# Halved first loads and a rewritten order of pieces in an attention and gated-convolution kernel

## The chip, the core and the metric

The kernel runs on one core of a Trainium2 chip. The metric is the device time of one execution in microseconds (us). Five engines work side by side: TensorE (PE in the profile, with its weight loads shown apart as PEld), VectorE (DVE), ScalarE (ACT), GpSimd (POOL) and SyncE (SP), which here does nothing but issue the transfers between main memory and the on-chip memory.

## The reference: what is computed

Four batches of 768 rows; 8 heads of 64. Attention inside a window, with 24 extra columns for block maxima of k and block means of v, feeds a gated convolution layer:

```python
k_sum = k.reshape(B, H, nb, block, D).max(axis=3)
v_sum = v.reshape(B, H, nb, block, D).mean(axis=3)
scores_l = scale * np.matmul(q, k.transpose(0, 1, 3, 2))
mask_l = np.abs(pos[:, None] - pos[None, :]) < window
scores_s = scale * np.einsum('bhsd,bhnd->bhsn', q, k_sum) + np.log(block)
scores_all = np.concatenate([np.where(mask_l, scores_l, -1e9), scores_s], axis=-1)
a = np.exp(scores_all - np.max(scores_all, axis=-1, keepdims=True))
a = a / (np.sum(a, axis=-1, keepdims=True) + 1e-09)
x = np.matmul(a, np.concatenate([v, v_sum], axis=2))      # then (B, S, H * D)
...
for k in range(K):                                        # K = 5
    gate_pre += conv_w[k][None, None, :] * xp[:, k:k + S, :]
gate = 1.0 / (1.0 + np.exp(-gate_pre))
val = x @ w_val
return (gate * val @ w_out).astype(np.float32)
```

## The kernel before

**Units and groups.** The rows are cut into 12 groups of 256 (a group is a batch and a third of its rows). A group has two units, one for each half of the four head pairs (`hp`), so there are 24 units; unit `u` belongs to group `u // 2`. A unit has two head pairs, `r` = 0 and 1.

**The order is written out by hand.** The text `ORDER` names some 1,275 pieces. They are recorded in that order, each engine runs its own pieces in the order in which they stand, and waits for the others by semaphores. A piece is a letter and its unit or group. For a unit: `s` scores (PE, L566, 16 matmul records for each head pair), `n` adds the mask and takes the row maximum (DVE, L581, eight instructions for a unit), `e` exponentials (ACT, L594, eight), `rr` and `rv` row sums and their reciprocals (DVE), `m` multiplies by them (POOL, L608), `t` transposes (PE, L618), `c` copies them out (ACT, or DVE as `cd`), `x` is the product with v (PE, L629 and L647), `Y` and `X` copy x, plain and rounded (ACT; `Yd`, `Xd` on DVE; `Xp` on POOL), `Z` makes the remainder of the rounding (POOL, L669), `I` and `T` are the five taps of the convolution (ACT or DVE `Id`, and DVE L685), `G` the gate (ACT). For a group: `v` is x times w_val (PE, L713), `gf` the gating (DVE), `gh`, `gl` its rounded part and remainder, `o` the product with w_out (PE, L753), `ob` copies it out and `O` stores it.

**What stands at the start.** `W` is a matmul on zeros whose result nobody reads (L335); `wz` clears its operand. `Lk`, `Lq`, `Lv`, `Ln`, `Lwv`, `Lc` load k, q, v, v again turned (vT), the four quarters of w_val and the taps' weights; batch 0 brings the queries of group 0 along with k. `ks` takes the block maxima of k (DVE, L258) and `kc` copies them into the columns that the scores read (POOL, L272). `vp` (DVE, L309) and `vt` (POOL, L318) sum blocks of vT, `vc` copies the sums, `vb` transposes them (PE, L345) and `vbc` puts them into `vblk`, which `x` of group 0 reads beside v. The weights come as 64-bit numbers and are made into 32-bit words: `rb` takes the high half (ACT, L387), `sh` the low bits (DVE, L392), `or` joins them into `wf` (DVE, L400); `wc` and `wl` split `wf` into a rounded part and a remainder. The scores of all units share one pair of PSUM banks, so `s` of a unit waits until all eight `n` of the unit before have read it. Group 0 multiplies by `wf` itself, in eight pieces of four matmul records; later groups use the two parts. `F` copies block means into a group's v by four small transfers (L369), and waits on SP until that v has landed.

Of the kernel before, what the change touches and what calls it, by code (L numbers as in the profile page):

```python
# [10 lines left out]
F32 = mybir.dt.float32  # L11
# [47 lines left out]
vp1.1 n1.1.1 e1.1.1 n1.0.0 n1.0.1 e1.0.1 t0.1 W33 c0.1 e1.0.0 orwv0 vp0.1 vp1.0 vp0.0 rr1 m0.0
t0.0 vt2.0 vc0.1 vc1.0 vt2.1 s2.1 s2.0 vc0.0 vc1.1 orc rv1 vb0 m1.0 n2.0.0 n2.1.1 n2.0.1 n2.1.0  # L60
c0.0 e2.0.0 e2.0.1 rbwv1 t1.0 e2.1.1 e2.1.0 c1.0 shwv1 vbcd0 orwv1 s3.0 s3.1 rbwv2 Lk1.0 x0.1
x0.0 Y0 m1.1 vt2.2 wcpwv0 wlwv0 t1.1 v0.1.0.0 n3.0.0 n3.1.1 n3.1.0 rr2 shwv2 n3.0.1 orwv2 I0.1
T0.1.0 rv2 T0.1.1 ks1.0 e3.0.0 e3.1.0 I0.0 e3.1.1 e3.0.1 c1.1 vt3.0 vt3.1 vt3.2 vt3.3 vt3.4
vc3.0 vt2.3 vt2.4 vc2.1 m2.1 vc3.1 vc2.0 m2.0 kc1.0 Lq2 s4.1 s4.0 Lwv3 Lv1 Lk1.2 Lk1.1 T0.1.2
n4.0.0 n4.1.0 n4.0.1 T0.0.0 n4.1.1 T0.0.1 shwv3 rr3 v0.0.1.0 v0.1.1.0 vb1 t2.1 e4.1.0 vbc1 s5.1
s5.0 T0.1.3 rv3 n5.1.0 T0.0.2 n5.0.0 T0.0.3 e4.0.0 e4.1.1 c2.1 rbwv3 x1.0 x1.1 Lk1.3 G0 Y1
# [60 lines left out]
v9.0.1 v9.0.0 T19.0.3 n23.0.1 T19.1.0 n23.1.1 e23.1.1 Xd21 rr22 T19.1.1 T19.1.2 T19.1.3 e23.0.1
# [14 lines left out]
def tile_attention_then_gated_conv(  # L142
# [746 lines left out]
```

## Time and profile before

| what | value |
|---|---|
| median of 3 runs | 234.44 us (234.27 to 234.57) |
| the profiled execution: its time, and its span | 233.49 us, 231.7 us |
| busy: PE, PEld, DVE, ACT, POOL | 97%, 83%, 86%, 71%, 73% of the span |
| moved by DMA | 46.20 MB |
| TensorE clock granted, mean | 0.998 of full |

The span is the stretch from the first to the last instruction in the trace; the 1.8 us between it and the execution's own time lie around it. Busy shares are means over the whole span, and a matmul's record is longer than its share of a run of matmuls, because they overlap; how fast PE goes is read from the distance between starts, or from the length of a run divided by its count.

### The profile page before, as it was taken

The numbers are of one execution on the slowest core, as the hardware profiler recorded it, in microseconds if no ns is written. First come the engines' busy times: TensorE is split into PE (matmuls) and PEld (weight loads), VectorE is DVE, ScalarE is ACT, GpSimd is POOL, SyncE is SP. The second block draws the span as 40 slices with busy tenths as digits, with TensorE's granted clock in tenths as the row PEclk, the third lists the DMA queues.
The fourth block names the chain that finished last, engine by engine and source line by source line (L and its number), as shares of the span: only waits on it lengthen the run. The fifth ranks groups of instructions, "written<-read, shape, count | busy, mean of one in ns | idle before, by whom it ended". The sixth has DMA issues, their size and how long they took to land.

```text
span 231.7 us, 8482 instructions
## 1 busy us (share of the span) xinstructions
PE 224.4 (97%) x3210; PEld 191.9 (83%) x3210; DVE 199.7 (86%) x743; ACT 165.4 (71%) x564; POOL 169.0 (73%) x257
## 2 busy tenths in 40 slices
PE   7988999999999999999999999999999999999994
PEld 2457798985798889998898898889998899879884
DVE  3699999999999999999999999978999987887610
ACT  2499999999999998689895575964856792543211
POOL 3289998888898989999989895884572945547220
PEclk9999999999999999999999999999999999999999
DMA  6999899999693983996834356102747230001052
GB/s 246 380 419 413 319 335 327 367 305 361 246 315 76 340 271 100 355 312 184 253 94 171 133 171 187 42 11 74 239 143 233 48 141 0 3 0 48 0 226 91
DMA packets 16167, 46.20 MB, mean 199 GB/s; under 512 B 2272, under 2 KB 2528, under 8 KB 16128
## 3 DMA queue, kind: packets, MB, share of 16 engines
q1 hardware_dynamic: 16128, 45.67, 57.0%
q8 instruction: 25, 0.41, 0.8%
q14 instruction: 14, 0.11, 0.2%
HBM read 37.21 MB, written 6.29 MB: 188 GB/s over the span
## 4 chain that ended last, share of the span: by engine, by line
PE 83%; DVE 11%; ACT 3%; issue 1%; POOL 0%; ACTq 0%; DVEq 0%; POOLq 0%
PE out L753 28%; PE val L713 25%; PE s L566 8%; PE pt L618 8%; PE x L629 7%; DVE g L685 4%; PE warm_out L335 3%; DVE sn L581 2%; PE x L647 2%; DVE wf L400 1%; DVE vpad L309 1%; ACT gt L692 1%; DVE ks L258 1%; PE vsp L355 1%; DVE gf L721 1%
## 5 line engine op out<-in xcount | busy, mean ns | idle before, releaser
L685 DVE SCALAR_TENSOR_TENSOR g<-xf,cwt,g 128x256 f32<-128x256 f32 x192 | 93.3, 486 | 7.3 <-ACT g L219 3.0
L594 ACT ACTIVATE p<-sn,nm 128x120 f32<-128x120 f32 x192 | 73.5, 388 | 8.9 <-DVE nm L581 7.6
L608 POOL TENSOR_TENSOR p<-p,ri 128x480 f32<-128x480 f32 x48 | 46.7, 987 | 14.6 <-DVE ri L604 11.6
L713 PE MATMUL val<-xh,wv 128*128 128x256 f32 x352 | 49.6, 284 | 0.0
L581 DVE CUSTOM_DVE_ANT_0 sn<-s,mask 128x120 f32<-128x120 f32 x192 | 43.7, 276 | 3.4 <-PE s L566 3.4
L753 PE MATMUL out<-wo,gh 128*128 128x512 f32 (+1 forms) x184 | 45.8, 390 | 0.3 <-ACT gh L726 0.3
L713 PEld LDWEIGHTS val<-xh,wv 128*128 128x128 f32 x352 | 44.3, 189 | 0.9 <-issue 0.2
L753 PEld LDWEIGHTS out<-wo,gh 128*128 128x128 f32 x184 | 32.4, 188 | 7.3 <-ACT gh L726 0.7
L669 POOL TENSOR_TENSOR xl<-xf,xh 128x512 fp32r<-128x512 f32 x22 | 28.2, 1287 | 12.6 <-ACT xh L656 6.9
L594 ACT ACTIVATION_READ_ACCUMULATOR p<-sn,nm 128x1 f32 x192 | 36.8, 192 | 0.0
L729 POOL TENSOR_TENSOR gl<-gf,gh 128x512 fp32r<-128x512 f32 x22 | 28.2, 1289 | 7.6 <-ACT gh L726 7.3
L621 ACT COPY pts<-pt 120x512 f32<-120x512 f32 x42 | 23.6, 578 | 10.1 <-PE pt L618 10.1
L692 ACT ACTIVATE gt<-g 128x512 f32<-128x512 f32 x24 | 14.3, 597 | 19.7 <-DVE g L685 19.7
L618 PE MATMUL pt<-ident,p 128*120 128x128 f32 x192 | 26.7, 274 | 1.3 <-POOL p L608 1.3
L713 PE MATMUL val<-xl,wv 128*128 128x256 f32 x176 | 27.6, 279 | 0.0
L286 POOL TENSOR_TENSOR vT<-vT 128x384 f32<-128x384 f32 (+3 forms) x44 | 25.0, 569 | 2.9 <-DMA vT<-in_vT_dram 0.3
L618 PEld LDWEIGHTS pt<-ident,p 128*120 128x120 f32 x192 | 21.7, 137 | 5.1 <-POOL p L608 2.2
L753 PE MATMUL out<-wo,gl 128*128 128x512 f32 (+1 forms) x92 | 23.8, 381 | 0.0
L566 PE MATMUL s<-k,q 64*64 64x120 f32 x704 | 23.3, 267 | 0.3 <-DVE g L685 0.3
L713 PEld LDWEIGHTS val<-xl,wv 128*128 128x128 f32 x176 | 23.6, 188 | 0.0
L566 PEld LDWEIGHTS s<-k,q 64*64 64x64 f32 x704 | 18.2, 133 | 3.0 <-issue 2.2
L219 ACT ACTIVATE ob<-out 128x512 f32<-128x512 f32 (+1 forms) x21 | 11.9, 574 | 11.2 <-PE out L753 7.2
(83 smaller groups left out, 327.5 us busy)
## 6 DMA issues: line engine op xcount, KB each, us to landing
v<-in_vw_dram SPq DMA_DIRECT2D x24, 512.0 KB
vT<-in_vT_dram SPq DMA_DIRECT2D x16, 384.0 KB
out_dram<-ob SPq DMA_DIRECT2D x23, 256.0 KB
k<-in_kT_dram SPq DMA_DIRECT2D x12, 478.0 KB
q<-in_qT_dram SPq DMA_DIRECT2D x11, 512.0 KB
k<-in_kq_dram SPq DMA_DIRECT2D x4, 606.0 KB
raw_wv<-in_wv_dram SPq DMA_DIRECT2D x4, 512.0 KB
raw_wo<-in_wo_dram SPq DMA_DIRECT2D x4, 512.0 KB
```

Source lines behind the costliest of these rows:

```text
L286: nc.gpsimd.tensor_tensor(dst, src[:, :, :n], src[:, :, n : 2 * n], ALU.add)
L566: nc.tensor.matmul(sp(u)[64 * e : 64 * e + 64, h, c * KW : c * KW + KW], qs[64 * h : 64 * h + 64, i * QT : i * QT + QT], ktile[b, pr][64 * ...
L581: nc.vector.tensor_tensor_reduce(sn(u)[:, n, :], sp(u)[:, h, c * KW : c * KW + KW], mask[:, mv, :], -1.0 / math.sqrt(D), 3.0e38, ALU.add, ...
L594: nc.scalar.activation(pr_(u)[:, n, :], sn(u)[:, n, :], AF.Exp, bias=nm(u)[:, n : n + 1], scale=-1.0, accum_out=rs(u)[:, n, 0:1],)
L608: nc.gpsimd.tensor_tensor(pr_(u)[:, w], pr_(u)[:, w], st["ri", u][:, w].unsqueeze(2).broadcast_to([P, TPU, KW]), ALU.mult,)
L618: nc.tensor.transpose(pt[:KW, i, :], pr_(u)[:, TPU * r + i, :], ident)
L621: (eng or nc.scalar.copy)(pts(u)[:, TPU * r : TPU * r + TPU], st.pop(("pt", u, r))[:KW])
L669: nc.gpsimd.tensor_tensor(xl(g)[:, two(hp), :], xf(g)[:, two(hp), HALO:], xh(g)[:, two(hp), :].bitcast(F32), ALU.subtract,)
L685: nc.vector.scalar_tensor_tensor(gp(u)[:, r], xf(g)[:, pr, o : o + SG], cwt[:, pr, o : o + 1], gp(u)[:, r], ALU.mult, ALU.add,)
L713: nc.tensor.matmul(pp[:, r], w, x, start=first and n == 0, stop=last and n == len(terms) - 1)
L729: nc.gpsimd.tensor_tensor(gl(g)[:, two(cp), :], grp["gf", g, cp], gh(g)[:, two(cp), :].bitcast(F32), ALU.subtract)
L753: nc.tensor.matmul(pp, x, w, start=start and n == 0, stop=stop and n == len(terms) - 1)
```

## The change

The loads of v of group 0 and of q of group 1 are each split by `hp`, so that unit 0 and unit 2 need only a first half. The low bits of one quarter of w_val are taken on POOL (`shpwv1`), by a multiplication and a minimum in place of a shift. `v0_sum` gets a parameter that no piece sets. All pieces stand in another order; there is one `W` less, and some copies and first taps change their engine. The matmuls that give results are the same.

```diff
 ORDER = """
-ez wz W0 W1 W2 W3 W4 W5 Mu Lk0.0 Lk0.1 Mm ks0.0 ks0.1 kc0.0 W6 W7 W8 W9 W10 W11 W12 W13 W14 W15
...
+ez hal0 Mu wz W0 W1 W2 W3 W4 W5 W6 W7 W8 W9 W10 W11 W12 Mm Lk0.1 ks0.1 Lk0.0 ks0.0 Mi kc0.1
...
-    def load_q(g):
+    def load_q(g, hp=None):
         b, th = divmod(g, NTH)
+        if hp is not None:
+            nc.sync.dma_start(qt(g)[:, two(hp)], qT[b, th][:, two(hp)])
+            return
         nc.sync.dma_start(qt(g), qT[b, th])
...
-    def load_v(g):
+    def load_v(g, hp=None):
         b, th = divmod(g, NTH)
-        t = ld.tile([VROWS, TPU, DM], F32, tag="v", name=f"v_{g}")
+        if g not in vtile:
+            vtile[g] = ld.tile([VROWS, TPU, DM], F32, tag="v", name=f"v_{g}")
+        t = vtile[g]
+        if hp is not None:
+            for e in range(VP):
+                nc.sync.dma_start(t[:, 2 * e : 2 * e + 2, half(hp)], vw[b, th, e][:, :, half(hp)])
+            return
...
     def low_bits(eng, dst, raw):
         low = raw.rearrange("p (n two) -> p two n", two=2)[:, 0]
+        if eng is nc.gpsimd:
+            eng.tensor_scalar(dst.bitcast(U32), low, 2.0**-29, 7.0, ALU.mult, ALU.min)
+            return
         eng.tensor_scalar(dst.bitcast(U32), low, 29, None, ALU.logical_shift_right)
```

**The loads.** SyncE's rows after the four loads of k (which stand first in both kernels), before the change; `wv0` to `wv3` are the quarters of w_val, `vT_0_2` is vT of batch 0 and head pair 2, `v_0` and `q_1` belong to groups 0 and 1:

```order
L451 DMA cwraw_177<-in_cw_dram 128x40
L415 DMA raw_wv0_179<-in_wv_dram 128x1024
L292 DMA vT_0_1_181<-in_vT_dram 128x768
L292 DMA vT_0_0_183<-in_vT_dram 128x768
L292 DMA vT_0_2_185<-in_vT_dram 128x768
L230 DMA q_1_187<-in_qT_dram 128x1024
L415 DMA raw_wv1_189<-in_wv_dram 128x1024
L249 DMA v_0_191<-in_vw_dram 128x1024 x2
L415 DMA raw_wv2_194<-in_wv_dram 128x1024
L292 DMA vT_0_3_196<-in_vT_dram 128x768
```

And of the change, in the same place:

```order
L300 DMA vT_0_1_177<-in_vT_dram 128x768
L300 DMA vT_0_0_179<-in_vT_dram 128x768
L300 DMA vT_0_3_181<-in_vT_dram 128x768
L462 DMA cwraw_183<-in_cw_dram 128x40
L231 DMA q_1_185<-in_qT_dram 128x512
L426 DMA raw_wv1_187<-in_wv_dram 128x1024
L426 DMA raw_wv0_189<-in_wv_dram 128x1024
L255 DMA v_0_191<-in_vw_dram 128x2x256 x2
L231 DMA q_1_185<-in_qT_dram 128x512
L426 DMA raw_wv2_320<-in_wv_dram 128x1024
L300 DMA vT_0_2_322<-in_vT_dram 128x768
L233 DMA q_2_324<-in_qT_dram 128x1024
```

The vT loads and half of q move up, v of group 0 comes with half its bytes; its other half follows behind `wv3`.

**PE behind x of unit 0.** PE's rows from that place on, before; `pt_1_1` is the transpose of unit 1 and head pair 1, `val_0_1` a piece of group 0's product with w_val, `s_4` the scores of unit 4:

```order
L618 MATMUL pt_1_1_438<-ident_100,p_1_278 120x128 x4
L713 MATMUL val_0_1_443<-xf_0_263,wf_108 128x256 x2
L566 MATMUL s_4_497<-k_0_1_130,q_2_495 64x120 x8
L566 MATMUL s_4_497<-k_0_0_128,q_2_495 64x120 x8
L713 MATMUL val_0_0_539<-xf_0_263,wf_108 128x256 x2
L713 MATMUL val_0_1_443<-xf_0_263,wf_108 128x256 x2
L345 MATMUL vb_1_544<-ident_100,vpad_103 128x128 x4
```

And of the change, behind x of unit 0:

```order
L577 MATMUL s_3_425<-k_0_3_175,q_1_185 64x120 x8
L577 MATMUL s_3_425<-k_0_2_173,q_1_185 64x120 x8
L629 MATMUL pt_1_0_451<-ident_100,p_1_275 120x128 x4
L724 MATMUL val_0_1_466<-xf_0_117,wf_108 128x256 x4
L724 MATMUL val_0_0_471<-xf_0_117,wf_108 128x256 x2
L629 MATMUL pt_1_1_474<-ident_100,p_1_275 120x128 x4
L577 MATMUL s_4_492<-k_0_1_144,q_2_324 64x120 x8
L577 MATMUL s_4_492<-k_0_0_148,q_2_324 64x120 x8
```

Three pieces of the product stand ahead of the scores of unit 4, where one stood (two rows are one piece); the scores of unit 3 stand behind x of unit 0 and stood ahead of it.

**DVE between the scores of units 2 and 3.** DVE's rows before; `sn_2` and `nm_2` are the masked scores and the maximum of unit 2:

```order
L581 ISA sn_2_347,nm_2_348<-s_2_320,mask_99 128x120
L581 ISA nm_2_348 128x1
L392 TENSOR_SCALAR wf_108<-raw_wv1_189 128x512
L222 TENSOR_SCALAR vb_105<-vb_0_341 120x2x256
L400 SCALAR_TENSOR_TENSOR wf_108<-sc_wv1_363,wf_108 128x512
L581 ISA sn_3_446,nm_3_447<-s_3_379,mask_99 128x120
```

And of the change:

```order
L592 ISA sn_2_348,nm_2_349<-s_2_302,mask_99 128x120
L592 ISA nm_2_349 128x1
L403 TENSOR_SCALAR wf_108<-raw_wv0_189 128x512
L615 RECIPROCAL ri_1_399<-ri_1_399 128x8
L411 SCALAR_TENSOR_TENSOR wf_108<-sc_wv0_374,wf_108 128x512
L411 SCALAR_TENSOR_TENSOR wf_108<-sc_wv1_376,wf_108 128x512
L671 COPY xf_0_117<-x_0_0_356 128x2x256
L403 TENSOR_SCALAR wf_108<-raw_wv2_320 128x512
L592 ISA sn_3_460,nm_3_461<-s_3_425,mask_99 128x120
```

Both quarters that the first pieces need are joined here, one of their low bits comes from POOL, the put into `vblk` has gone to ACT, and the copy of x has come from ACT.

## Rows read from the trace of the kernel before

**Rows 1.** The page: busy time by engine, and the costliest group (busy us, mean ns).

```profile
PE 224.4 (97%) x3210; PEld 191.9 (83%) x3210; DVE 199.7 (86%) x743; ACT 165.4 (71%) x564; POOL 169.0 (73%) x257
...
L685 DVE SCALAR_TENSOR_TENSOR g<-xf,cwt,g 128x256 f32<-128x256 f32 x192 | 93.3, 486 | 7.3 <-ACT g L219 3.0
```

**Rows 2.** The chain in order of time: start us, us, what.

```profile
17.68 0.20 DVE sn L581
...
24.80 1.05 PE s L566 x32
...
216.04 1.42 PE val L713 x12
217.46 11.05 PE out L753 x60
228.58 0.38 ACT ob L219
```

**Rows 3.** PE's timeline: start us, us; in brackets idle before it.

```profile
1.53 6.77 PE L335 MATMUL warm_out<-warm 128*128 128x512 bf16 x22 [1.53 <-POOL warm L330]
8.23 0.64 PE L566 MATMUL s<-k 64*64 64x120 f32 x16
...
20.30 0.33 PE L647 MATMUL x<-pts,v 120*64 120x64 f32 x2
...
22.58 0.65 PE L618 MATMUL pt<-ident,p 128*120 128x128 f32 x4
23.32 1.13 PE L713 MATMUL val<-xf,wf 128*128 128x256 f32 x4
...
33.08 2.76 PE L713 MATMUL val<-xf,wf 128*128 128x256 f32 x12
...
36.64 1.05 PE L566 MATMUL s<-k,q 64*64 64x120 f32 x32
```

**Rows 4.** The timeline of PE's weight loads: the last slow one, then the quick ones.

```profile
4.91 0.15 PEld L335 LDWEIGHTS <-warm 128*128 128x128 bf16 x1 [0.28 <-issue]
5.33 2.47 PEld L335 LDWEIGHTS <-warm 128*128 128x128 bf16 x12 [0.27 <-issue]
```

**Rows 5.** DVE's timeline.

```profile
5.76 0.95 DVE L258 TENSOR_REDUCE ks<-k 128x24 f32<-128x768 f32 x1 [0.53 <-DMA k<-in_kq_dram]
8.94 0.28 DVE L581 CUSTOM_DVE_ANT_0 sn<-s,mask 128x120 f32<-128x120 f32 x1 [2.23 <-PE s L566]
...
19.02 0.89 DVE L392 TENSOR_SCALAR wf<-raw_wv 128x512 uint32<-128x512 uint32 x1
19.83 0.68 DVE L222 TENSOR_SCALAR vb<-vb 120x512 f32<-120x512 f32 x1
20.43 0.68 DVE L400 SCALAR_TENSOR_TENSOR wf<-sc_wv,wf 128x512 uint32<-128x512 uint32 x1
```

**Rows 6.** ACT's timeline.

```profile
21.84 0.65 ACT L387 ACTIVATE sc_wv<-raw_wv 128x512 f32<-128x512 f32 x1
```

**Rows 7.** POOL's timeline.

```profile
1.51 0.53 POOL L195 IOTA lag<- 128x120 f32 x3
...
13.67 1.93 POOL L608 TENSOR_TENSOR p<-p,ri 128x480 f32<-128x480 f32 x2 [0.68 <-DVE ri L604]
...
40.91 2.53 POOL L669 TENSOR_TENSOR xl<-xf,xh 128x512 fp32r<-128x512 f32 x2 [0.70 <-ACT xh L656]
```

**Rows 8.** POOL's groups by line: busy us, mean ns of one, idle before.

```profile
L440 POOL TENSOR_TENSOR wv<-wf,wv 128x512 fp32r<-128x512 f32 x4 | 5.1, 1274 | 0.2
...
L437 POOL CAST wv<-wf 128x512 fp32r<-128x512 f32 x4 | 2.4, 610 | 0.0
```

**Rows 9.** Windows: us, busy PE, PEld, DVE, ACT, POOL, PEclk, DMA share, GB/s.

```profile
20.00:25.00 5.00, 4.56 (x96) 3.60 (x92) 5.00 (x25) 4.81 (x20) 4.41 (x7) 1.00 1.04 421
...
25.00:45.00 20.00, 20.00 (x333) 17.66 (x327) 19.77 (x91) 19.20 (x71) 18.67 (x35) 1.00 0.93 336
...
165.00:185.00 20.00, 20.00 (x294) 18.10 (x294) 19.07 (x63) 13.35 (x49) 12.03 (x15) 1.00 0.56 171
```

**Rows 10.** SyncE's timeline: time to issue.

```profile
28.93 3.46 SPq L369 DMA_DIRECT2D v<-vb  x4
```

More of the change, by code (lines that the diff above doesn't have):

```diff
@@ new lines @@
+s12.1 T6.0.1 rr10 rv10 T6.0.2 T6.0.3 Y8 ob2.1 Ya8 n12.0.1 tv2.3 Z6 m9.1 o2.0 Z7 Lu2.1 Lk3.3
+Lk2.2 ks2.2 ks2.3 kc2.3 kc2.2 O1.1 Lu2.2 Lv5 F5 t9.1 t9.0 v3.0.1 v3.1.0 G6 e11.1.0 X8 I7.0 c9.1
+e11.0.0 e12.0.1 c9.0 e11.0.1 x9.1 Id7.1 T7.0.0 n12.1.1 T7.0.1 n12.1.0 T7.1.0 n12.0.0 T7.0.2
+T7.1.1 T7.0.3 T7.1.2 T7.1.3 e11.1.1 e12.0.0 tv2.2 hal4 s13.0 x9.0 Y9 m10.1 Z8 Ya9 m10.0 G7 Lk3.0
+Lk3.1 O1.0 s13.1 n13.0.0 n13.1.0 v3.0.0 I8.0 gf3.0 Id8.1 v3.1.1 t10.0 t10.1 X9 Z9 n13.0.1 T8.0.0
+rr11 e12.1.0 e12.1.1 rr12 T8.0.1 T8.0.2 n13.1.1 gf3.1 T8.1.0 T8.1.1 T8.1.2 rv11 c10.0 c10.1
@@ new lines @@
+c12.1 Xp11 tv3.3 Z11 Z10 gl4.0 s16.0 s16.1 x12.1 x12.0 e14.0.1 e14.1.0 e14.0.0 ob3.0 T10.0.3
+rr14 m13.1 n16.1.1 n16.1.0 n16.0.1 G10 e15.1.1 I11.0 Y12 e15.0.1 m13.0 ks3.2 rv14 Ya12 n16.0.0
+Xd12 m14.1 v5.1.0 v5.0.1 t13.1 t13.0 v5.0.0 ob3.1 e15.1.0 I11.1 c13.0 cd13.1 x13.1 x13.0 Y13
+T11.1.0 T11.0.0 T11.0.1 T11.1.1 T11.1.2 kc3.0 gl4.1 m14.0 hal6 Z12 s17.0 s17.1 e15.0.0 e16.0.0
+gf5.0 T11.1.3 Ya13 T11.0.2 T11.0.3 n17.0.1 ks3.3 rr15 X13 G11 v5.1.1 o4.1 I12.1 I12.0 n17.1.1
+T12.0.0 T12.1.0 T12.1.1 T12.0.1 T12.0.2 rv15 T12.0.3 n17.1.0 gf5.1 Z13 tv3.2 ob4.1 t14.0 t14.1
@@ new lines @@
+o4.0 m15.0 v6.0.1 v6.1.1 v6.0.0 m15.1 kc3.3 n17.0.0 T12.1.2 cd14.1 T12.1.3 gh5.0 e16.1.0 e16.1.1
+e17.0.1 e17.1.1 gh5.1 e16.0.1 gl5.0 gl5.1 kc3.2 e17.1.0 G12 cd14.0 I13.0 I13.1 ks3.1 kc3.1
+T13.0.0 T13.0.1 T13.1.0 gf6.0 t15.1 c15.1 Lv8 F8 O3.1 O3.0 Lq10 Lu3.1 Lq9 Lv7 F7 Lu3.0 O0.0
+tv3.1 t15.0 c15.0 s18.0 s18.1 x14.0 x14.1 Y14 n18.1.1 n18.0.0 e17.0.0 ob4.0 e18.1.1 n18.0.1
+e18.0.1 e18.0.0 Ya14 T13.1.1 T13.0.2 rr16 rv16 n18.1.0 T13.1.2 o5.1 x15.0 x15.1 s19.1 s19.0
+v6.1.0 ob5.1 T13.0.3 Yd15 rr17 Ya15 T13.1.3 G13 e18.1.0 tv3.0 hal7 ghp6.0 m16.1 m16.0 I14.0
@@ new lines @@
+t16.1 t16.0 c16.1 I14.1 n19.1.0 n19.0.1 n19.1.1 gf6.1 rr18 T14.1.0 T14.1.1 rv17 T14.1.2 n19.0.0
+T14.1.3 T14.0.0 c16.0 X14 o5.0 x16.1 x16.0 s20.0 s20.1 e19.1.0 e19.0.1 Y16 e19.0.0 hal8 Xd15
+gl6.0 m17.1 ghp6.1 Z14 gl6.1 Ya16 n20.0.1 m17.0 T14.0.1 n20.1.1 n20.1.0 rv18 T14.0.2 T14.0.3 G14
+o6.0 t17.1 t17.0 vsp3 c17.0 n20.0.0 cd17.1 Z15 Xp16 s21.0 s21.1 x17.1 x17.0 e20.0.1 ob5.0
+e20.0.0 vscd3 e19.1.1 Id15.0 Id15.1 T15.1.0 T15.1.1 T15.1.2 m18.0 T15.0.0 Y17 Ya17 T15.1.3
+T15.0.1 T15.0.2 T15.0.3 rr19 G15 v7.0.0 v7.1.0 v7.1.1 v7.0.1 m18.1 t18.1 t18.0 O4.0 Lv9 O4.1 F9
@@ new lines @@
+rv19 n21.0.1 n21.1.1 gf7.1 ob6.0 Lv10 O5.1 Lq11 F10 O6.0 e20.1.0 I16.0 e20.1.1 Id16.1 T16.0.0
+rr20 T16.0.1 T16.1.0 rv20 T16.1.1 T16.1.2 c18.0 c18.1 Xp17 hal9 Z17 Z16 v8.0.0 v8.1.1 x18.0
+x18.1 e21.1.1 Y18 T16.1.3 T16.0.2 m19.1 m19.0 T16.0.3 m20.1 n21.1.0 G16 Ya18 I17.1 v8.1.0 v8.0.1
+t19.0 t19.1 I17.0 n21.0.0 T17.0.0 gf8.0 e21.0.1 c19.0 c19.1 s22.1 s22.0 x19.0 x19.1 e21.1.0
+e21.0.0 T17.1.0 gf7.0 ghp7.0 T17.1.1 T17.1.2 T17.0.1 T17.0.2 n22.1.1 T17.0.3 Xp18 m20.0 gh7.1
+gl7.1 gl7.0 n22.1.0 T17.1.3 Y19 Ya19 rr21 G17 gf8.1 n22.0.1 I18.0 o6.1 o7.0 t20.1 t20.0 o7.1
@@ new lines @@
+I18.1 e22.1.1 c20.0 e22.0.1 c20.1 T18.0.0 T18.0.1 rv21 T18.1.0 m21.1 obd7.0 n22.0.0 T18.0.2
+T18.1.1 Xd19 hal10 ghp8.0 m21.0 gl8.0 Z18 Z19 T18.1.2 t21.0 t21.1 c21.0 c21.1 gh8.1 gl8.1 s23.1
+s23.0 T18.1.3 T18.0.3 G18 I19.0 obd7.1 I19.1 x21.1 x21.0 Y21 n23.0.0 T19.0.0 T19.0.1 n23.0.1
+T19.1.0 x20.1 x20.0 Y20 T19.1.1 T19.1.2 T19.1.3 T19.0.2 T19.0.3 v9.1.0 o8.1 v9.1.1 X20 e23.0.1
+e22.0.0 obd8.1 e22.1.0 n23.1.0 rr22 rv22 O5.0 ob6.1 O6.1 O7.0 O7.1 Lv11 F11 X21 G19 Id20.1
+n23.1.1 e23.1.1 T20.1.0 v9.0.0 v9.0.1 T20.1.1 e23.1.0 I20.0 T20.0.0 e23.0.0 T20.0.1 rr23 T20.0.2
@@ L138 @@
+gf11.0 T23.1.3 v11.1.1 v11.1.0 ghp11.0 G23 gl11.0 o10.0 O9.0 ob10.0 O8.0 O8.1 gf11.1 ob10.1
+ghp11.1 gl11.1 o11.0.1 obd11.0.1 O11.0.1 O10.1 O9.1 O10.0 o11.1 ob11.1 O11.1 o11.0.0 ob11.0.0
+O11.0.0
 """
```

136 lines of the change are left out of this document (48 added, 88 removed).

## The prediction

> **What bounds the kernel now.** I read the busy shares first: PE has work in 97% of the span, DVE in 86% [rows 1]. A mean over stages with different limits says little, so the windows came next: from 25 us on PE is busy in all of the stretches shown, 20.00 of 20.00 us [rows 9]. Then the chain: it enters PE for good at 24.80 with the scores of unit 4, and its last stretch on PE is 11.05 us of the output product from 217.46 on; after that only a copy at 228.58 and a store are left [rows 2]. So the end is the moment from which PE is never short of work, plus the PE work still to do, plus some 3 us of copy and store. No result-giving matmul is added or removed, so the question is how much of that work PE has done when it stops starving.
>
> What starves it before 24.80? PE's timeline begins with 22 matmuls on zeros, 1.53 to 8.23, and only then come the first scores [rows 3]. DVE, idle for 2.23 us, begins masking them at 8.94 [rows 5] and from there has no gap: five of five us in the window 20 to 25 [rows 9]. PE waits for its results: x of unit 0 from 20.30, the first piece of group 0's product at 23.32, the scores of unit 4 at 24.80 [rows 2, 3].
>
> **Part 1: the first scores.** In the order of the change 13 of the matmuls on zeros, not 22, stand ahead of them, and the operand is cleared behind POOL's iota (0.53 us [rows 7]), so they start some 0.55 later, at 2.08. The weight loads show two paces: at 4.91 and 5.33 the starts are 0.42 apart, from 5.33 on 12 take 2.47, 0.21 each [rows 4]: 512 columns at 1.2 and at 2.4 GHz. Nine were slow (1.53 to 5.33, 3.8 us). With nine slow and four quick ones: 2.08 + 3.8 + 4 x 0.21 = 6.7, with a first weight load 6.8, against 8.23. The first of the two k blocks has been reduced by 5.2 (the reduction of the second waits for its load until 5.76 [rows 5]) and put in place by POOL at 5.7, so it isn't late. DVE can mask from about 7.45 (scores 0.57, a semaphore 0.1), **1.5 us earlier**.
>
> **Part 2: DVE up to the scores of unit 4.** These wait for all eight maskings of unit 3. Before, DVE took 24.80 - 8.94 = 15.86 us. In that run the change takes out the low bits of one quarter (0.81 from start to start, 19.02 to 19.83), the put into `vblk` (0.60, 19.83 to 20.43) [rows 5] and one join (0.60, it stands later now), and puts in the copy of x (taken as 0.60, like the put of the same 512 columns). Maskings at 0.20 [rows 2], reductions, block sums and two taps are the same. 15.86 - 0.81 - 0.60 - 0.60 + 0.60 = 14.45. Walked piece by piece, DVE also waits about 1.0: 0.3 around the first maskings, 0.4 for x of unit 0, 0.3 for the scores of unit 3. 7.45 + 14.45 + 1.0 = 22.9.
>
> **Part 3: PE up to there.** x of unit 0 needs four things. Its transposes: POOL's multiplication starts 12.1 (13.67 before [rows 7], less the 1.5). The block sums: DVE has them at 14.85, POOL's copies at 15.75, the transposes on PE at 16.25, ACT's put at 16.9. The half of v: 5.52 MB stand up to it in the queue, 6.30 before; the second k block (1.24 MB) had landed by 5.76 [rows 5] and the rate is 421 GB/s [rows 9], so it lands near 5.76 + 4.28 / 0.421 = 15.9 instead of 17.8. The put is the last, so x runs from 16.95, not 20.30, for 2.1 (20.30 to about 22.4 [rows 3]). Then scores of unit 3 (0.98), a transpose (0.45), three pieces of the product, of which 12 records take 2.59 (33.08 to the next group [rows 3]; 0.86 a piece), another transpose (0.5): 19.05 + 0.98 + 0.45 + 2.6 + 0.5 = 23.6. DVE is ready at 22.9, so unit 4's scores start at **23.6**, with three pieces done where one was: 24.80 - 23.6 + 2 x 0.86 = **2.9 us ahead**. The same walk to the scores of unit 6 (36.64 before [rows 3]) has DVE ready at 33.55 and PE there at 33.7 with the same seven pieces done: 2.9 again.
>
> **Prices that no row shows.** The low bits on POOL: a cast of 512 columns takes 0.61, a two-operand operation 1.27 [rows 8]; the bounds are nothing (if hidden) and twice the dearer, 2.5. I take 1.0, as it has one operand but two operations. It starts near 16.3; its join on DVE also waits for two conversions on ACT (0.57 each, from one of 0.65 with overlap [rows 6]) which end at 18.5, so up to 2.2 it costs nothing, and beyond that it delays the first pieces one for one: 0 to 0.3. The half loads: pieces of 1 KB in place of 4 KB a partition. From below nothing; from above the poorer 336 GB/s at a share of 0.93 in 25 to 45 [rows 9], 361 at full share, makes 1.05 MB cost 2.9 instead of 2.5. I take 0.2 for the first half; the load has 1.0 to spare against the put, so nothing. By the Trainium skill ("DMA: Bandwidth & Descriptors", section Bandwidth) halving is a loss: a transfer of 1 MB reaches 341 GB/s and one of 64 KB 138, so batch to 1 MB or more; an estimate at the smaller figure would make the 0.52 MB land 2.5 us later and x of unit 0 start near 18.5. The rows disagree: 384 to 512 KB transfers queued one behind the other run at 421 GB/s here [rows 9]. Block means for group 1 (`F`): v of group 1 stands at 9.8 MB, landing near 26.1, then 3.46 to issue [rows 10], landed by 31; x of unit 2 comes at 34.7. Hidden, with 3.7 to spare.
>
> **Part 4: from there to the end.** POOL must give remainders of x in time for group 1's product. Before, the two ended at 40.91 + 2.53 = 43.4 [rows 7], and the product, begun 42.5, needs the second about 0.95 later: just in time. In the change POOL starts 1.57 earlier, sheds two casts (1.2 [rows 8]) and two copies of k maxima (0.8), had idle time of 1.2, and gains the low bits (1.0): 3.8 earlier, about 39.6 to 40.2, where PE begins at 38.7 and needs it at 39.65. I take **0.4 lost** (0 to 0.6). Later DVE has 0.93 idle in 165 to 185 and 0.23 in 25 to 45 [rows 9], and a dozen first taps go from it to ACT: it can follow. For small waits in the new order 0.1. The end, copy and store, is as long as before.
>
> Sum: 2.9 - 0.4 - 0.1 = 2.4. Against its own execution 233.49 - 2.4 = 231.1. That stands 0.95 under the median of the runs, so I forecast **232.0** for the median. A difference of 0.2% (0.47 us) is about what can be told from none.
>
> **The rivals.**
> - *The lead can't be kept* (0.14). DVE and POOL are 99% and 93% busy in 25 to 45 [rows 9], and they start only 1.5 earlier. If PE must fall back to them, the gain is 1.5 less the 0.4 and 0.1: 1.0, 233.4. Against it: the walk has DVE ready before PE at units 4 and 6, because pieces left it.
> - *POOL is as late as it was* (0.08). If the low bits and what was moved about it leave the remainders at 43.4, the product of group 1 starts no earlier and nothing is gained: 234.4, no change. It needs POOL to lose 3.8 us, against a dearest price of 2.5.
> - *The clock* (0.05). PEclk reads 1.00 in the rows, but the pace doubled only at 5.33 [rows 4]. If it doesn't double in the first 10 us now, the 13 take 5.5, scores take 0.8 and the eight before unit 1's scores are slow too: these come at 12.6 instead of 10.0, and 0.2 of the gain is left, 234.2. Against: PE is busy from 2.08 to 9.7 almost without a gap.
> - *Slower: the taps at the end* (0.11). Behind x of unit 23 PE has four whole output products (2.76 each: 11.05 is worth four) and four pieces at 1.42 [rows 2] before the last gated part is read, and 0.95 more before its remainder is: 17.6 us. In that time DVE has 18 taps at 0.49 [rows 1], four first taps (0.5), four gatings and a copy (0.6), then come a gate (0.6), a cast (0.61) and a remainder (1.27 [rows 8]), with 0.6 for semaphores: 16.8. A backlog B at that point costs B - 0.8, and from B = 3.7 the kernel is slower than before; with 4.3 it takes 235.5. For it: 0.93 idle in 20 us is little [rows 9]; against: taps have gone to ACT, busy 13.35 of 20.
> - Otherwise as forecast (0.62): 230.9 to 233.0. The lower end is the full 3.35 by which x of unit 0 moves, with 0.2 on top.
>
> **How the numbers follow.** Faster: the forecast, and the first rival, 0.62 + 0.14 = 0.76. Same: POOL and the clock, 0.13. Slower: 0.11. The range runs from 230.9 up to 234.4, which takes in all but the slower case and a bit below.
>
> **What would show it.** Part 1: the first scores near 6.8, DVE's first masking near 7.45. Part 2: POOL's operation on the low bits under 2.2 and no wait of the join. Part 3: x of unit 0 from 16.95 without a wait for v, the scores of unit 4 near 23.6 with three pieces ahead. Part 4: PE's wait in group 1's product under 0.6, and the last output matmul 2.4 earlier than before. I am wrong if PE's waits behind 25 us come to more than 1 us, on POOL's remainders, on the scores held by DVE, or on the last gating; or if the first scores come after 7.6.

## The result: slower by 1.0 to 1.7%, where a gain of 1% was forecast

The change takes 236.90 us (median of 4 runs, 236.37 to 238.13), and the kernel before, run between them on the same chip, 234.50 us (median of 4, 234.27 to 238.76). The ratio is 1.0136, 95% interval [1.0101, 1.0170]: 2.4 to 4.0 us slower; the two medians lie 2.4 apart. The prediction was 232.0 us, with 0.76 on faster. The profiled execution took 236.37 us, its span is 234.3. Ratios, this one and those below, are against runs of the kernel before on the same chip, and leave out an execution that took over 1.5% longer than the fastest of its kernel, as the 238.76 here.

**Busy time and PE's waits.** The page of the change (busy time), which answers to [rows 1], then its waits of PE (us in total, times, longest):

```profile
PE 224.9 (96%) x3209; PEld 192.1 (82%) x3209; DVE 199.4 (85%) x738; ACT 167.5 (71%) x568; POOL 171.1 (73%) x258
```

```profile
PE s L577 <- DVE nm L592: 1.0, 2, 0.6
PE val L724 <- DVE xf L671: 0.8, 1, 0.8
PE val L724 <- POOL xl L680: 0.4, 1, 0.4
PE x L658 <- DMA v<-in_vw_dram: 0.4, 1, 0.4
PE pt L629 <- ACT pts L632: 0.4, 1, 0.4
```

PE and DVE do as much as before; ACT and POOL do 2.1 us more each, of 234. What is longer is the time in which PE has nothing to do (9.4 us of its span, 7.3 before); behind its start, 3.4 of that are waits of 0.2 to 0.8 (2.2 before).

**The chain in order of time**, for [rows 2]:

```profile
2.89 7.19 DMA vT<-in_vT_dram
10.09 8.41 DMA v<-in_vw_dram
...
21.85 0.69 DVE xf L671
...
149.98 1.50 DVE xh L667
...
213.39 1.27 POOL xl L680
```

Before, it was on PE from 24.80 until the taps near the end. Now it starts with two loads, and leaves PE again at 20.2 and near 142. The load of v that ends at 18.50 is the half that unit 0 waits for. The end is alike in both: the prediction has the chain before enter PE "for good" at 24.80, but between the rows of [rows 2] it left it once more, for taps and gatings from 187.91 on, and came back at 207.07:

```profile
187.91 0.60 ACT ob L219
...
206.40 0.63 ACT gh L726
```

In the change it is off PE near the end from 207.53 to 214.70.

**PE's timeline**, for [rows 3]:

```profile
2.14 5.25 PE L343 MATMUL warm_out<-warm 128*128 128x512 bf16 x13 [2.14 <-POOL warm L338]
7.32 0.64 PE L577 MATMUL s<-k 64*64 64x120 f32 x16
...
17.29 0.33 PE L658 MATMUL x<-pts,v 120*64 120x64 f32 x2
...
18.55 0.34 PE L658 MATMUL x<-pts,v 120*64 120x64 f32 x4 [0.39 <-DMA v<-in_vw_dram]
...
20.15 1.05 PE L577 MATMUL s<-k,q 64*64 64x120 f32 x32
...
22.59 2.86 PE L724 MATMUL val<-xf,wf 128*128 128x256 f32 x12 [0.81 <-DVE xf L671]
...
25.82 1.05 PE L577 MATMUL s<-k,q 64*64 64x120 f32 x32
...
31.41 1.05 PE L577 MATMUL s<-k,q 64*64 64x120 f32 x32 [0.59 <-DVE nm L592]
...
37.06 1.05 PE L577 MATMUL s<-k,q 64*64 64x120 f32 x32
```

The scores of unit 4 start at 25.82 (24.80 before [rows 2]), with three pieces of the product done where one was: 2 x 0.86 - 1.02 = 0.7 us ahead, not 2.9. At the scores of unit 6 (37.06 against 36.64 [rows 3], seven pieces done in both) PE is 0.4 behind.

**The pace**, for [rows 4]: the last slow weight load on zeros, and the first scores after it.

```profile
6.38 0.15 PEld L343 LDWEIGHTS <-warm 128*128 128x128 bf16 x1 [0.28 <-issue]
6.79 0.10 PEld L343 LDWEIGHTS <-warm 128*128 128x128 bf16 x1 [0.26 <-issue]
7.32 0.41 PEld L577 LDWEIGHTS s<-k 64*64 64x64 f32 x16 [0.42 <-issue]
```

Here eleven starts lie 0.43 apart (512 columns at 1.2 GHz), where before nine did, so the first scores came 0.5 later than forecast.

**DVE, ACT and POOL about x of unit 0**, for [rows 5], [rows 6] and [rows 7]; three timelines:

```profile
8.03 0.28 DVE L592 CUSTOM_DVE_ANT_0 sn<-s,mask 128x120 f32<-128x120 f32 x1 [0.91 <-PE s L577]
...
17.52 0.42 DVE L403 TENSOR_SCALAR wf<-raw_wv 128x512 uint32<-128x512 uint32 x1
...
18.45 1.33 DVE L411 SCALAR_TENSOR_TENSOR wf<-sc_wv,wf 128x512 uint32<-128x512 uint32 x2 [0.40 <-ACT sc_wv L395]
21.85 0.69 DVE L671 COPY xf<-x 128x512 f32<-128x512 f32 x1 [2.06 <-ACT g L219]
```

```profile
20.26 0.45 ACT L219 ACTIVATE g<-x,cwt 128x256 f32<-128x256 f32 x1 [0.47 <-PE x L660]
20.63 0.38 ACT L605 ACTIVATE p<-sn,nm 128x120 f32<-128x120 f32 x1
...
21.39 0.43 ACT L219 ACTIVATE g<-x,cwt 128x256 f32<-128x256 f32 x1
```

```profile
12.89 1.93 POOL L619 TENSOR_TENSOR p<-p,ri 128x480 f32<-128x480 f32 x2 [0.90 <-DVE ri L615]
...
16.96 1.97 POOL L401 TENSOR_SCALAR wf<-raw_wv 128x512 uint32<-128x512 uint32 x1
```

x of unit 0 is done by 20.2, and DVE is free at 19.8; yet it copies x only at 21.85, behind the *second* of ACT's two taps on the same x (21.39 + 0.43). Between the two taps ACT does two exponentials. All three instructions only read x, but they read one PSUM tile from two engines, and the copy stands behind the taps in the order: it carries a wait for ACT. Before, ACT made the copy itself, first. The low bits on POOL took 1.97, twice the 1.0 taken.

**The windows**, for [rows 9], in the stretch with the least room, and SyncE's row that answers to [rows 10]:

```profile
25.00:45.00 20.00, 18.81 (x302) 16.09 (x301) 20.00 (x80) 18.69 (x67) 16.78 (x26) 1.00 0.85 306
```

```profile
28.78 3.96 SPq L377 DMA_DIRECT2D v<-vb  x4
```

DVE is busy in all of the 20 us, and PE, which was busy in 20.00, is now so in 18.81. Issuing the block means took 0.5 longer, and no wait of PE follows from it.

### The profile page after: what moved, and what is told of

It reads as the page before. It is cut to its first block, busy times and chain, and to the rows that moved or that the text cites. A ratio compares the mean times of both kernels' runs of the same rounds, so it can differ in the third digit from the quotient of the medians.

```text
span 234.3 us, 8466 instructions
## 1 busy us (share of the span) xinstructions
PE 224.9 (96%) x3209; PEld 192.1 (82%) x3209; DVE 199.4 (85%) x738; ACT 167.5 (71%) x568; POOL 171.1 (73%) x258
## 4 chain that ended last, share of the span: by engine, by line
PE 73%; DVE 10%; DMA 7%; ACT 6%; POOL 1%; issue 1%; SPq 1%; DVEq 0%; ACTq 0%
PE val L724 26%; PE out L764 25%; PE pt L629 7%; PE x L640 6%; PE s L577 6%; DMA v<-in_vw_dram 4%; DVE g L696 3%; DMA vT<-in_vT_dram 3%; ACT p L605 2%; PE x L658 2%; DVE sn L592 2%; SPq L238 1%; ACT g L219 1%; ACT pts L632 1%; ACT xf L671 1%
## 5 line engine op out<-in xcount | busy, mean ns | idle before, releaser
L740 POOL TENSOR_TENSOR gl<-gf,gh 128x512 fp32r<-128x512 f32 x22 | 28.7, 1307 | 5.5 <-ACT gh L737 5.0
L764 PEld LDWEIGHTS out<-wo,gl 128*128 128x128 f32 x92 | 16.9, 188 | 3.4
```

The source lines that it names most:

```text
L740: nc.gpsimd.tensor_tensor(gl(g)[:, two(cp), :], grp["gf", g, cp], gh(g)[:, two(cp), :].bitcast(F32), ALU.subtract)
L764: nc.tensor.matmul(pp, x, w, start=start and n == 0, stop=stop and n == len(terms) - 1)
```

## The experiments

To compare kernels whose orders differ, PE's result-giving matmuls were added up in each trace, each with the mean distance between starts of its kind. The table gives by how many us a kernel reaches the same sum later than the kernel before (- is earlier), at the moments named above. Where kinds of matmul stand in another sequence it swings by some tenths. Its early columns also hold something that is not the order's: the moment at which PE's pace doubles differs from one execution to the next, from 4.5 to 8.1 us in the fourteen traces, and with it the first scores, which came at 6.43 to 7.80 with the start of the change and at 7.84 to 9.10 with that of before. e4, at 7.79, is one of the late ones.

```
                                 25     30     36     45     60    110    140    170    225 us
change                         -0.6   -0.7   +0.5   +0.8   +0.8   +0.8   +1.4   +2.0   +2.1
e1 copy first                  -2.1   -1.7   -1.0   -0.8   +0.3   +0.4   +1.2   +1.8   +1.9
e2 v first                     -0.2   -0.3   +1.2   +1.6   +1.6   +1.6   +2.1   +2.7   +2.8
e3 bits on DVE                 -0.7   -0.8   +0.4   +0.9   +0.9   +0.9   +1.7   +2.5   +2.7
e4 all three                   -1.2   -1.2   +0.4   +0.7   +0.7   +0.7   +1.6   +2.3   +2.5
x1 start of change             -0.7   -0.7   +0.8   +2.0   +1.8   +1.6   +1.6   +1.8   +1.8
x2 rest of change              -0.3   -0.4   -0.4   +1.0   +1.5   +0.8   +1.5   +2.2   +2.3
x3 best start, then before     -2.4   -2.0   -0.1   +0.8   +0.5   +0.3   +0.3   +0.5   +0.5
b1 halves alone                +0.5   +0.9   +0.9   +0.8   +0.5   +0.5   +0.5   +0.5   +0.6
x4 change up to 113            -1.0   -1.1   +0.1   +0.5   +0.5   +0.5   +4.2   +4.4   +4.4
x5 change from 110             -0.1   +0.2   +0.2   +0.2   +0.9   +0.9  +11.9  +12.6  +12.7
x7 rounding on ACT             -0.4   -0.4   +1.1   +1.4   +1.4   +1.4   +2.0   +2.0   +2.2
```

**The copy ahead of the taps.** One piece of the change is moved:

```diff
-s3.1 s3.0 e2.1.1 I0.1 e2.0.0 I0.0 e2.1.0 t1.0 rbwv2 Yd0 shwv2
+s3.1 s3.0 e2.1.1 Yd0 I0.1 e2.0.0 I0.0 e2.1.0 t1.0 rbwv2 shwv2
```

> One piece of the changed kernel moves: DVE's copy of x of unit 0 stands ahead of ACT's first taps, which read the same PSUM tile, instead of behind them. In the changed kernel DVE stood idle 2.06 us and began that copy at 21.85, 1.6 us behind the last matmul of x. Theory A (the time is lost in the first 40 us, and what is won there arrives at the end): the copy begins near 20.3, PE's wait of 0.8 for it goes, the scores of unit 4 start 0.8 to 1.4 earlier (25.8 before the edit) and the kernel gets 0.8 to 1.4 us faster, about 235.2. Theory B (from unit 5 on the other engines set the pace, so a lead is eaten again): the scores of unit 4 come earlier too, but those of unit 6 (37.1) and the end move by less than 0.3.

235.98 us, ratio 1.0093 [1.0060, 1.0127]. Two timelines of it, DVE's and PE's:

```profile
19.98 0.68 DVE L667 COPY xf<-x 128x512 f32<-128x512 f32 x1
```

```profile
21.21 2.76 PE L720 MATMUL val<-xf,wf 128*128 128x256 f32 x12
...
24.54 1.05 PE L573 MATMUL s<-k,q 64*64 64x120 f32 x32
```

The copy runs at 19.98 with no wait (ACT's first tap now waits 0.64 for it): the wait at 21.85 was the order's. PE reaches the scores of unit 4 at 24.54, 2.0 us ahead of before. By 60 us that lead is gone (-0.8 at 45, +0.3 at 60; at 53 PE waits 1.1 for a copy of x on DVE), and the last copy comes at 230.44 against 230.62: of 1.3 us won, 0.2 is left in these two traces. So the wait was real, and most of what its removal gains is lost again; whether some of it stays, the times don't tell (1.0093 against 1.0136, with intervals that overlap).

**The half of v sooner, the low bits back on DVE, and all three.** In the change:

```diff
-Lq1.0 Lwv1 Lwv0 Lv0.0 Lq1.1
+Lq1.0 Lv0.0 Lwv1 Lwv0 Lq1.1
```

```diff
-vt3.1 shpwv1 orwv1 vt3.2
+vt3.1 shwv1 orwv1 vt3.2
```

> One piece moves: the first half of v of group 0 is loaded ahead of the two quarters of w_val (0.52 MB each) that stood in front of it. In the changed kernel x of unit 0 waited for it until 18.55, though its other inputs were there at about 17.4. Theory A: x starts at 17.4 to 17.6, as the load now lands near 16; the quarters land 1.3 later, which delays the join on DVE (18.45) by up to 0.8; net 0.3 to 0.8 us faster, about 235.8. If the load were not what x waits for, its start would stay at 18.5. Theory B: x is earlier by 1.0, the end moves by less than 0.3.

> The low bits of one quarter of w_val go back to DVE, in the same place of the order (the computation is unchanged). On POOL they took 1.97 us, on DVE 0.4 to 0.9. POOL's next multiplication (19.35) starts 1.5 to 2.0 earlier, and the block sums behind it (25.3) and unit 2's multiplication (26.6) with them if DVE isn't what they wait for. Theory A: 0 to 0.6 us faster, as the join and the copy of x behind it are held by DVE's wait for ACT anyway, and PE waits for POOL nowhere before 30. Theory B: no change within 0.3. If POOL is what costs the lead between 28 and 36, the scores of units 5 and 6 come at least 0.8 earlier.

> All three edits at once: copy of x ahead of the taps, first half of v ahead of the quarters, low bits on DVE. Theory A: x of unit 0 from about 17.5, scores of unit 4 near 23.8 (25.8 in the changed kernel), those of unit 6 near 35, and 1.5 to 2.2 us faster at the end: 234.2 to 234.9, level with the kernel before. Theory B: the same early lead, but unit 6 above 36.5 and an end above 235.9.

Ratios 1.0147 [1.0121, 1.0173], 1.0099 [1.0068, 1.0129] and 1.0101 [1.0064, 1.0137]. Neither the load nor POOL's 1.97 us is the cause alone: with v first, x of unit 0 starts at 17.30 and runs through, but DVE waits 1.14 for a quarter of w_val instead, its copy of x comes at 22.26, and PE waits 1.8 for it. All three together are no better than the copy alone.

**Which part of the order.** Two kernels join the orders just ahead of x of unit 2 (about 38 us): the change up to there and then the pieces in the order of before (x1), and the reverse (x2).

```diff
-(before up to x2.1)  (rest in the order of before)
+x1: (change up to x2.1)  (rest in the order of before)
+x2: (before up to x2.1)  (rest in the order of the change)
```

> The order of the change up to x of unit 2 (all that runs in the first 40 us), then the remaining pieces in the order and on the engines of the kernel before. In the changed kernel PE had the same work done 0.5 to 0.8 us later than the kernel before at 36 to 45 us, 0.8 at 120, 1.7 at 160, 2.1 at 225, and the stretch behind PE's last copy was 0.5 longer. Theory L (most is lost by the later order): this kernel stays at 0.5 to 0.9 behind and ends 0.5 to 1.0 slower than before, about 234.9 against 234.1. Theory S (the start sets the loss, what shows later follows from it): it ends 1.8 or more slower, as the change does, about 236.

> The reverse: the kernel before up to x of unit 2, full loads and all, then the remaining pieces in the order and on the engines of the change. Theory L: level with before up to 45 us, then behind by 0.9 to 1.3 at 160 and 1.2 to 1.8 at the end: 235.3 to 235.9 against 234.1. Theory S: within 0.5 of the kernel before.

x1 took 235.62 and 235.95 us, 1.0075 [1.0045, 1.0104], and x2 236.36, 1.0102 [1.0069, 1.0135]. The joint itself costs both of them 1 to 1.5 us at 36 to 45, so the totals say little. The slopes behind it do: x1 loses nothing from 60 to 225 us, x2 loses 1.4 from 110 to 170, as much as the change (1.2).

**The best start with the later order of before.** e1 up to the scores of unit 5, then the order of before:

> The order of the change with DVE's copy of x ahead of the taps, up to the scores of unit 5, then the remaining pieces as in the kernel before. That start had PE 2.0 us ahead of the kernel before at 25 to 28 us. Theory K (a lead can be kept): PE stays 1.5 or more ahead to 120 us and the kernel ends 1.2 to 2.0 faster than before, about 232.5. Theory B (DVE, ACT and POOL have no room between 25 and 60 us, so PE falls back to them): the lead shrinks to 0.7 or less by 60 us and the end is within 0.7 of the kernel before.

235.0 us (median of 10), 1.0037 [1.0015, 1.0059]. PE's waits in it, and its timeline:

```profile
PE val L720 <- ACT xf L667: 1.6, 1, 1.6
PE s L573 <- POOL k L276: 0.7, 1, 0.7
```

```profile
24.05 1.05 PE L573 MATMUL s<-k,q 64*64 64x120 f32 x32
...
32.88 2.86 PE L720 MATMUL val<-xf,wf 128*128 128x256 f32 x12 [1.61 <-ACT xf L667]
35.58 1.04 PE L625 MATMUL pt<-ident,p 128*120 128x128 f32 x8
37.27 1.05 PE L573 MATMUL s<-k,q 64*64 64x120 f32 x32 [0.66 <-POOL k L276]
```

Here PE is 2.4 us ahead at 25 us, near the 2.9 of the forecast. It stands still for 1.6 on ACT and 0.7 on POOL, and at the scores of unit 6 it is 0.6 behind (37.27 against 36.64 [rows 3]). From there on nothing more is lost. The trace is of the fastest of the ten runs, 234.08 us. Five had a mean granted clock of 0.998 or more and took 234.08 to 234.92; the other five, at 0.990 to 0.993, took 235.07 to 235.59. So part of x3's time is a lower clock, which this trace doesn't show.

**The wait on ACT taken away.** In x3 the copy of x of unit 1 is moved up on ACT, behind that x:

```diff
-x1.1 x1.0 T0.1.1 ... c2.1 Lk1.3 G0 Y1 wcpwv2 I1.1
+x1.1 x1.0 Y1 T0.1.1 ... c2.1 Lk1.3 G0 wcpwv2 I1.1
```

> The kernel that began as the change with the copy of x of unit 0 ahead of the taps and went on as before, with one piece moved: ACT's copy of x of unit 1 stands at once behind that x, ahead of ten pieces of ACT, so that PE's wait of 1.6 us for it at 31.3 goes. Theory P (a piece stood in the wrong place, the engines have the room): most of that 1.6 is kept, PE is 1.5 ahead at 40 us and the time is 233.4 to 233.8, under the kernel before at 234.1. Theory B (no room on DVE, ACT and POOL between 25 and 45 us): the wait goes to the next pieces, PE is level again by 45 us, and the time stays at 234.5 to 235.0.

Four runs took 236.15 to 237.81, ratio 1.0151 [1.0100, 1.0203]: slower than x3, which neither theory foresaw. The lead is not kept by moving the piece that PE waits for. The trace is of a fifth and longer run (240.88), so its times are not to be compared, but it shows a next wait, for POOL's copy of k maxima ahead of the scores of unit 6:

```profile
38.98 1.88 PE L573 MATMUL s<-k,q 64*64 64x120 f32 x32 [2.12 <-POOL k L276]
```

These scores take 1.88, 1.05 in x3: with that wait the granted clock fell, to a mean of 0.73 from 37 to 41 us. The mean clock of all five runs is 0.984 to 0.993, where the kernel before has 0.997 to 1.000, so a lower clock has a part in x6's time; how large it is isn't told.

**The loads in halves alone.** The order of before, with the four half loads in place of the two whole ones:

```diff
-Lq1 ... Lv0
+Lq1.0 Lq1.1 ... Lv0.0 Lv0.1
```

> One part of the change alone, on the kernel before: v of group 0 and q of group 1 come in halves, the second half right behind the first, nothing else moved. If 1 KB pieces and more transfers are dear, v of group 0 lands 0.5 to 2.5 later than before (20.1) and x of unit 0 starts later than 20.3 by as much, with up to 1 us at the end. If they are nearly free, x of unit 0 starts within 0.4 of 20.3 and the end is within 0.3 of before.

234.72 us, 1.0028 [1.0006, 1.0050]: 0.1 to 1.2 us lost. Its weight loads on zeros and its PE:

```profile
7.05 1.62 PEld L339 LDWEIGHTS <-warm 128*128 128x128 bf16 x8 [0.28 <-issue]
```

```profile
9.10 0.64 PE L573 MATMUL s<-k 64*64 64x120 f32 x16
...
21.19 0.33 PE L654 MATMUL x<-pts,v 120*64 120x64 f32 x2
```

x of unit 0 is 0.89 late (20.30 [rows 3]), but the first scores are already 0.87 late (8.23), since here the pace doubled at 7.05 and not at 5.33 [rows 4]. The half of v that this x reads had landed by 17.7 (the whole by 20.1 before). So what the trace has lost by 25 us is that moment's doing, and it shows no price of the halves; what the 0.3% in the times comes from stays open. The halves gain nothing without an order that uses them.

**The later order, cut at unit 12.** The change up to the scores of unit 16 and then before (x4), and before up to the transposes of unit 12 and then the change (x5):

> The order of the change up to the scores of unit 16 (some 113 us in), then the order of the kernel before for all that is left. In the change the transposes of unit 12 stood at 110.51 us and before at 109.72, so 0.8 was lost by there, and 1.25 more up to the last copy (230.62 against 228.58). Theory L (the later order of the change loses of itself): what is lost by 113 us stays at 0.8 to 1.0, the last copy is near 229.5 and the time near 235.0 where the kernel before takes 234.1. Theory S (the loss behind 113 us is what the start did to the engines that follow, and comes whatever the order): 236.2 or more, like the change.

> The order of the kernel before up to the transposes of unit 12 (some 110 us in), then the order of the change. Theory L: level with the kernel before up to 110 us, then 1.0 to 1.3 later, most of it between 110 and 170 with a wait of PE for the maskings of DVE near 153; time near 235.3 where the kernel before takes 234.1. Theory S: 234.1, no difference.

238.52 us, 1.0199 [1.0154, 1.0243], and 246.40, 1.0520 [1.0463, 1.0576]. Both theories missed: the joints cost 3.7 and 11 us by 140 us, since pieces that one order had put ahead of the cut and the other behind it now come too late (x5: PE waits 5.4 us for POOL's remainders). As tests of the totals they failed. Behind the joint, from 140 to 225 us, x4 loses 0.2 and x5 0.8, as the change does (0.7).

**One named piece of the later loss.** In the change the rounded copy of x of unit 15 goes from DVE to ACT:

```diff
-e19.0.0 hal8 Xd15 gl6.0 m17.1
+e19.0.0 hal8 X15 gl6.0 m17.1
```

> The change with one piece on another engine: the rounded copy of x of unit 15 on ACT (busy 5.4 of 10 us there) in place of DVE, where it took 1.5 us at 149.98 with the maskings of unit 20 behind it. Theory L1 (that piece is the later loss): PE's wait of 0.4 for the maskings at 155 goes, and with it 0.5 to 0.9 of the time: 235.4 to 235.8 where the change takes 236.3. Theory L2 (many small waits): 236.2 to 236.4.

236.38 us, 1.0104 [1.0062, 1.0146]. PE's timeline there, in the change and in x7:

```profile
155.21 1.12 PE L577 MATMUL s<-k,q 64*64 64x120 f32 x30 [0.40 <-DVE nm L592]
```

```profile
155.34 1.05 PE L573 MATMUL s<-k,q 64*64 64x120 f32 x32
```

In the change the chain comes to this row through the 1.50 of `xh` on DVE at 149.98. In x7 the wait is gone, and from 110 to 170 us it loses 0.6 where the change loses 1.2. So this piece makes about half of the later loss, as far as one trace of each can tell. Against the change in time it can't be told from none (1.0104 and 1.0136, with intervals that overlap): its profiled run had lost 0.6 more by 45 us.

## Why the prediction was wrong

**Where its sum broke.** The last copy was forecast 2.4 us earlier and came 2.04 later (230.62 against 228.58 [rows 2]), 4.4 apart. By the places: 2.2 at the scores of unit 4 (0.7 ahead, not 2.9), 1.0 from there to 110 us (1.5 lost where 0.5 was forecast), 1.2 from 110 to 170.

**Part 1** held but for the clock: 7.32, not 6.8, within the 7.6 it allowed. The eleven slow starts are what differs from [rows 4]; how many there are is the execution's, not the order's (6.43 to 7.80 above). **Part 2** failed in one sentence: "a copy of x (taken as 0.60, like the put of the same 512 columns)". The copy has that length (0.6 from its start to the next), but it waited until 21.85 for ACT's taps. A piece that goes to another engine was costed by its duration, and its new wait was not looked for. **Part 3**'s "The put is the last" was wrong: the load was. x began at 17.29 for 16.95, and then the second transfer of the half of v was missing until 18.5, not 15.9: x ended at 20.2 instead of 19.05, 1.1 late. The load's time was worked out as bytes by 421 GB/s from 5.76. The same sum gives 17.8 for the kernel before, where the load landed at 20.1, so the trace of before could have shown what it leaves out. In the change the second k block had landed at 6.17, and from there the page has 410 and then 380 GB/s in its slices:

```profile
GB/s 239 410 380 408 414 174 380 219 365 251 285 264 315 215 225 129 200 345 233 261 138 338 88 141 164 107 10 157 213 102 1 3 120 200 31 0 137 0 41 183
```

With slices of 5.86 us the same 4.28 MB are through at 17.0 (2.27 MB by 11.71, the other 2.01 MB at 380). The last 1.5 lies within the spread of the load itself: the trace has sixteen completions for it, the first at 16.29, the fourteenth at 17.03, and then 17.43 and 18.51. In that stretch a packet of another queue, `instruction`, ran 0.93 us from 16.48 on (the DMA view of 16.4 to 17.5 us, with one packet of 0.02 MB and its share of 16 engines):

```profile
q8 instruction: 1, 0.02, 5.3%
```

Up to it the sixteen completions of a load lie 1.1 to 1.3 apart, and from this load on 1.9 to 2.2. All fourteen traces have this step, each at its own first such packet. No run moves the packet alone, so that it makes the step is an inference. Of the 2.2 at unit 4, x makes 1.1, the wait for the copy 0.8, and small steps 0.3. The Trainium skill's "DMA: Bandwidth & Descriptors", section Bandwidth, by which smaller transfers lose, was set aside on the 421 GB/s; its figures are for transfers that GpSimd issues, and here SyncE does. The estimate by it, x near 18.5, is where x went on, but by chance: the bytes came at 380 to 410 GB/s, not at 138, and b1's trace shows no loss by the halves.

**The price of POOL's low bits** was 1.97, above the 1.0 taken and inside its bounds; under 2.2, as was said, it was not what held anything: e3, without it, is not told apart from the change (1.0099 against 1.0136, intervals overlapping).

**Part 4**'s remainders for group 1, forecast to start at 39.6 to 40.2, 3.8 earlier than before, started at 40.40 and 41.87 and ended at 43.17, 0.2 earlier (43.4 [rows 7]). No wait of PE came of it, since the product began only at 42.37.

**What met the lead is the first rival**, "the lead can't be kept", at 0.14. The argument against it was a walk that had DVE ready before PE at units 4 and 6. In e1 and x3 PE has the lead of 2.1 to 2.4 at 25 us, and nothing of it is left at 60 and 36. In e1 the three engines that feed PE are full from 25 to 45 us, fuller than in [rows 9], and PE is not:

```profile
25.00:45.00 20.00, 19.28 (x300) 16.53 (x293) 19.91 (x83) 20.00 (x72) 19.08 (x32) 1.00 0.85 313
```

In x3 they are not full (DVE 18.58, ACT 18.67, POOL 17.87 of 20): there they wait for each other in an order that was written for other times, DVE 1.29 us for POOL's copy of k maxima. That x6 took the largest of the new waits away and met another, of 2.1 us, fits the second. That these engines' work leaves no room for the lead in any order is not shown; what is shown is that none of the orders tried kept it. The rival's own time, 233.4, was too low, since it kept 1.0 of the lead.

**The loss from 110 to 170 us** had no place in the prediction beyond "0.1 for small waits". It comes with the later order: six more kernels that have it (e1 to e4, x2, x7) lose 0.6 to 1.6 there, and three that have the order of before from 60 us on (x1, x3, b1) lose 0.0 to 0.2. About half is DVE's rounding of x of unit 15, by x7. The other half shows as no wait of PE, and stays open. The rival of the taps at the end did not come: PE waits there 0.4, for a remainder on POOL at 214 (0.3 before, for a rounding on ACT at 207).

**Behind the last copy** the span goes on for 3.7 us, 3.1 before. Kernels with the tail of before show 3.1 to 3.7 too (x3 3.3, b1 3.7) and one with that of the change 3.1 (x2), so this 0.5 is no effect of the change. With it and 0.3 outside the span, the 2.04 at the last copy make the 2.9 between the two profiled executions (236.37 against 233.49).

## What to carry to other kernels

A lead that one engine is given is worth what the engines that feed it can follow: read their busy shares in the stretch behind it first, and where they are nearly full, as here (99%, 96% and 93%), don't count on the lead before a run has shown it. A load's landing that is worked out from bytes and a rate should first be worked out for a load whose landing the trace of before has. When a reader of a PSUM tile goes to another engine, look at what else reads that tile ahead of it in the order, and let the copy that others wait for be first. An order of hundreds of pieces that runs close on all engines is not joined to another one for nothing: cutting two such orders together cost 1 to 11 us here, so parts of it are better tested by moving one piece.

## What the runs showed of the hardware

- Two engines that read one PSUM tile are held in the order of the program here: DVE's copy waited 1.6 us for ACT's taps, and none once it stood ahead of them; then ACT's first tap waited 0.64 for the copy (e1).
- The sixteen completions of a load don't come together, and a consumer waits for the last: x of unit 0 went on at 18.55, behind the one at 18.51. In the change they lie 0.5 to 0.7 us apart for loads that end before 12.5 us, 1.1 to 1.3 at 13 to 17, 1.9 to 2.2 from 18 to 32. In all fourteen traces the spread grows by 0.7 to 1.5 us behind the first 16 KB packet of the queue `instruction`, which starts between 16.1 and 18.5 (before: 1.0 to 2.4 behind 16.73; b1: 0.5 to 1.7 behind 17.97).
- With PE on zeros from 1.5 or 2.1 us on, its pace doubled between 4.5 and 8.1 us in the fourteen traces, and the same start had its first scores at 6.43 to 7.80.
- A multiplication with a minimum on 512 32-bit integers a partition took POOL 1.97 us; the shift in its place takes DVE 0.4 to 0.9.
- In x5 PE waited 5.4 us. The granted clock was 0.80 and 0.63 in the 6 us windows from 118 and from 124, means between its levels of 1.2 and 2.4 GHz, and eight records of `val` took 1.91 us there and 1.19 ahead of it:

```profile
112.00:118.00 6.00, 5.30 (x116) 4.46 (x115) 4.27 (x16) 3.59 (x13) 1.57 (x5) 1.00 0.88 290
118.00:124.00 6.00, 0.57 (x4) 0.37 (x4) 4.35 (x18) 4.47 (x17) 5.38 (x8) 0.80 0.00 0
124.00:130.00 6.00, 6.00 (x35) 6.00 (x36) 1.52 (x3) 0.59 (x1) 5.75 (x8) 0.63 0.00 0
```

```profile
117.14 1.19 PE L720 MATMUL val<-xh,wv 128*128 128x256 f32 x8
123.77 1.22 PE L720 MATMUL val<-xl,wv 128*128 128x256 f32 x4 [5.43 <-POOL xl L676]
124.79 1.91 PE L720 MATMUL val<-xh,wv 128*128 128x256 f32 x8
```
